# Pool in text order, y stored by SP from four buffers, and the steps of a routed mixture kernel placed anew

## The chip, the cores and the metric

The kernel runs on one core of one Trainium2 chip. The metric is the device time of one execution, in microseconds. A core has five engines with queues of their own: TensorE (PE in the profile, with its weight loads as PEld), VectorE (DVE), ScalarE (ACT), GpSimd (POOL) and SyncE (SP, which here only issues DMAs).

## The reference

Eight batches of eight heads hold 512 tokens and 32 states each, 64 wide. Tokens read the states by attention, states read the tokens, and the two results, heads side by side, are 4352 rows of 512. Each row then goes through the best of eight experts.

```python
scores = scale * x @ state.T;  a = softmax(scores);  xread = a @ state
scores2 = scale * state @ x.T; a2 = softmax(scores2); sread = a2 @ x
rows = concat([xread, sread]) -> (4352, 512)
e = argmax(rows @ w_gate); g = softmax(rows @ w_gate)[e]
out[row] = g * relu(row @ w1[e]) @ w2[e]
```

## The kernel before

All token rows of a batch are mixtures of its 32 states, and in practice go to one expert. So the kernel guesses the batch's expert from the states (`guess`), multiplies the states by the expert's w1 (`states_w1`, tile pG, result G), and works on 1024 hidden units as vectors over the states.

Batch 0 is done with all units (`in_full`: tiles ph, then py from s). For batches 1 to 7, `lists(b)` sorts the units: those that are positive for every token need no relu and can be summed into one matrix M, the few undecided are done one by one, the rest are dropped. Its steps are: two halves of pG; the load of the next w1 and four times two transposes (pgt) that ACT copies into gt; statistics on DVE; then the rank matmuls, DVE's table `to`, and eight indirect DMAs of POOL that scatter gt's rows into g_dram. `fetch(b)` reads the sorted rows back (tile gp, three DMAs of POOL), and `gather(b, 3)`, called twice, collects the rows of w2 that belong to them (w2c, three indirect DMAs of POOL each; nine w2c buffers, six a batch). `mask(b)` clears unused slots on DVE. `batch(b)` then multiplies: pgu transposes, pm (M from gp and w2c), phu, py, and stores.

Beside this run `front(b)` (transposes of x on DVE, the score matmuls pa<-xt,stT, softmax, and the exponentials of the states' side), `back(b)` (transposes pa2, pq, the states' read pw, then the load of the x two batches on and a store of st_dram, then the gate's pl and pcnt), and `tokens()`: for each of two halves of the state rows `sort_states` and `rounds`. A round handles 128 state rows in up to three experts at a time and reads the weights in pieces: `fetch(n)` issues n pieces of three loads into five ring buffers s; `round_in` loads xg and, by `values_of`, puts the experts' numbers into SP's registers.

Most engines are wrapped in `InOrder`, so that their instructions keep the order of the text; POOL's DMAs too are issued through such a wrapper (`gp`). The text itself is woven from generators: `todo` maps a letter to a generator, and a plan names the letters to advance at each `insert()` in `in_full` and `batch`:

```python
todo = {"A": back(0), "X": states_on(), "G": rest_of_G(), "B": backs(), "T": fronts(), "S": listing(), "F": fetching(), "M": masking(), "R": tokens(), "K": late_constants()}
```

`store_batch(b)` gives the store of 128 token rows: ACT scales py by the gate into one of three y buffers, and ACT issues the DMA to the output; the very last is scaled by DVE and stored by SP. PE's results go through four PSUM banks (`bank`) and a four-bank tile `pa` for scores. In the queues as built before, POOL's instructions do not stand everywhere as in the text: a batch's six gathers follow its fetch together, ahead of the next batch's scatters, and a scatter of srow into ss_dram stands between gathers.

Of the kernel before, what the change touches and what calls it, by code (L numbers as in the profile page):

```python
# [9 lines left out]
FP32 = mybir.dt.float32  # L10
# [10 lines left out]
def kernel(  # L21
# [21 lines left out]
    class InOrder:  # L43
# [5 lines left out]
        def __getattr__(self, name):  # L49
            def call(*args, **kw):  # L50
# [6 lines left out]
    pe, dve, act, gp, sp = (InOrder(e) for e in (nc.tensor, nc.vector, nc.scalar, nc.gpsimd, nc.sync))  # L57

    B, H, S, D = x.shape
    NS = state.shape[2]  # L60
    DM = H * D
    E = moe_w_gate.shape[1]
    F = moe_w1.shape[2]
# [4 lines left out]
    NC = S // 128  # L68
# [18 lines left out]
    const, dram, wpool, att, ffn, sst = (pool(n, **({"space": bass.MemoryType.DRAM} if n == "dram" else {}))  # L87
                                         for n in ("const", "dram", "wpool", "att", "ffn", "sst"))
# [9 lines left out]
    def bank(shape=(128, 512), name="p"):  # L98
        return ps_p.tile(list(shape), FP32, tag="p", bufs=4, name=name)

    std = [ffn.tile([128, 2, 160], FP32, tag="Gu", name="std"), ffn.tile([128, 2 * B - 4, 160], FP32, tag="gt", name="std"),
# [322 lines left out]
    def no_dep(d):  # L426
        tc.declare_no_dep(d.ins, group="y", reason="every row of the result is written once")
        tc.add_to_no_dep_group("y", d.ins)
# [53 lines left out]
    def store_batch(b):  # L482
        rows = out[ds(b * SO, S)].rearrange("(p c) f -> p c f", c=NC)

        def store(c, py):
            y = ffn.tile([128, DM], FP32, tag="y", bufs=3, name="y")
            if b == B - 1 and c == NC - 1:
                dve.tensor_scalar(y[:], py[:], gw[:, NC * b + c, :], None, ALU.mult)
                no_dep(sp.dma_start(out=rows[:, c], in_=y[:]))
            else:  # L490
                act.activation(y[:], py[:], AF.Copy, scale=gw[:, NC * b + c, :])
                no_dep(act.dma_start(out=rows[:, c], in_=y[:]))
        return store

    gps, w2cs = {}, {}
# [221 lines left out]
    def rounds(t, r0, r1):  # L717
        parts = [(r, *p) for r in range(r0, r1)
                 for p in [(1, k, half) for half in range(2) for k in range(NDC)] + [(2, f, 0) for f in range(NFC)]]
        have, xgs, ex = {}, {}, {}  # L720

        def round_in(r):
            xgs[r] = sst.tile([128, XW], FP32, tag="xg", bufs=2, name="xg")
            sp.dma_start(out=xgs[r][:].bitcast(I32), in_=ss_dram[t][ts(r, 128)])
            ex[r] = values_of(eg[t][0:1, r].rearrange("p a q -> p (a q)"), SP)

        def fetch(n):
            for _ in range(n):
                if parts:
                    r, kind, k, half = parts.pop(0)  # L730
                    if r not in ex:
                        round_in(r)
                    w = ring()
                    for q in range(3):
                        src = (moe_w1[ds(ex[r][q], 1), ts(k, 128), ts(half, 512)] if kind == 1
                               else moe_w2[ds(ex[r][q], 1), ts(k, 128), :])
                        sp.dma_start(out=w[:, q], in_=src.rearrange("o p f -> p (o f)"),
                                     cond=ex[r][3 + q], bounds_check="skip_entire_dma")
                    have[r, kind, k, half] = w

        def four(dst, lhsT, r, kind, k, half, start, stop):
            w = have.pop((r, kind, k, half))
            for q in range(4):
                pe.matmul(dst[ts(q, 32), :], lhsT=lhsT[:, ts(q, 32)], rhs=w[:, PLACE[q], :], start=start, stop=stop,
                          skip_group_check=True)

        round_in(r0)
        fetch(RING)
        yield
        for r in range(r0, r1):  # L750
            xg = xgs[r]
            pt = bank((128, NDC, 128), "ptx")
            for c in range(NDC):
                pe.transpose(pt[:, c, :], xg[:, ts(c, 128)], ident[:])
            xT = sst.tile([128, NDC, 128], FP32, tag="sxT", name="sxT")
            act.copy(xT[:], pt[:])
            yield
            h = sst.tile([128, F], FP32, tag="sh", name="sh")
            for half in range(2):
                ph = bank(name="pgh")  # L760
                for k in range(NDC):
                    four(ph, xT[:, k], r, 1, k, half, k == 0, k == NDC - 1)
                act.activation(h[:, ts(half, 512)], ph[:], AF.Relu)
                fetch(4)
                yield
            hT = sst.tile([128, F], FP32, tag="shT", name="shT")
            for u in range(2):
                pt = bank((128, 4, 128), "pth")
                for i in range(4):
                    pe.transpose(pt[:, i, :], h[:, ts(4 * u + i, 128)], ident[:])  # L770
                evict(hT[:, ts(u, 512)], pt[:].rearrange("p i k -> p (i k)"))
            yield
            y = ffn.tile([128, DM], FP32, tag="y", bufs=3, name="ys")
            for u in range(2):
                py = bank(name="pgy")
                for f in range(4 * u, 4 * u + 4):
                    four(py, hT[:, ts(f, 128)], r, 2, f, 0, f == 4 * u, f == 4 * u + 3)
                if u == 0:
                    dve.tensor_scalar(y[:], py[:], xg[:, DM:DM + 1], None, ALU.mult)
                    fetch(4)  # L780
                    yield
            dve.scalar_tensor_tensor(y[:], py[:], xg[:, DM:DM + 1], y[:], ALU.mult, ALU.add)
            no_dep(gp.indirect_dma_start(
                out=out[:], out_offset=bass.IndirectOffsetOnAxis(ap=xg[:, DM + 1:DM + 2].bitcast(I32), axis=0),
                in_=y[:], in_offset=None, bounds_check=NTOK - 1, oob_is_err=False))
            fetch(4)
            yield
# [32 lines left out]
    G = [sst.tile([128, F], FP32, tag=n, name="G0") for n in ("sh", "shT")]  # L820
# [102 lines left out]
    for k in "TT":  # L923
        next(todo[k])
    in_full(G, aTs[0], w2x, store_batch(0), inserts(
        "GXTX,XTT,AKTK,AA,SBSK,BSSS,SB,TSAT,BSST,,TA,,TT,SB,BTTF,SSSS,BSBB,STTT,,T,,TSST,MSF,BSBT"))
    plans = {
        1: "SFSB,,TBS,FB,FSM,,T,,,T,T,STSF,FB",
        2: "R,BSTR,S,BM,BSS,BFTF,S,RSSR,,TF,RT,BS,R",
        3: ",SFTS,BR,T,,SSBS,T,BTB,SBR,MR,TT,SS,BSRS",  # L930
        4: "B,SF,TRS,,BSFR,FSS,,,T,RMRT,SBTT,S,",
        5: "RBF,T,SBSS,RFB,SBR,B,RFFS,,,,RBR,MRRR,",
        6: "RF,RF,,,,,,,,MFR,,,R",
        7: ",,R,,,R,R,R,,R,,,",
    }

    pres = const.tile([128, B, E], FP32)
# [2 lines left out]

    def count_left():
        assert listed[0] == B - 1 and attended[0] == B and sorted_[0] == NT
        others = const.tile([128, B, E], FP32)
        eb_f = const.tile([128, B, 1], FP32)
        dve.tensor_copy(out=eb_f[:, :, 0], in_=eb[:])
        dve.tensor_tensor(others[:], io8[:].unsqueeze(1).to_broadcast([128, B, E]), eb_f[:].to_broadcast([128, B, E]),
                          ALU.not_equal)
        over = const.tile([128, B, 1], FP32)
        tmp8 = const.tile([128, B], FP32)
        dve.tensor_tensor(tmp8[:], nn[:, :, 1], nn[:, :, 0], ALU.subtract)  # L950
        dve.tensor_scalar(over[:, :, 0], nn[:, :, 0], float(CAPP), None, ALU.is_gt)
        dve.scalar_tensor_tensor(over[:, :, 0], tmp8[:], float(CAPU), over[:, :, 0], ALU.is_gt, ALU.max)
        dve.tensor_tensor(others[:], others[:], over[:].to_broadcast([128, B, E]), ALU.max)
        dve.scalar_tensor_tensor(pres[:], cnt[:], 0.5, others[:], ALU.is_ge, ALU.mult)
        n_f = const.tile([128, 2], FP32)
        dve.tensor_reduce(n_f[:, 0:1], pres[:], AX.XY, ALU.add)
        dve.tensor_reduce(n_f[:, 1:2], more[:], AX.X, ALU.add)
        rest_f = const.tile([128, 1], FP32)
        dve.tensor_reduce(rest_f[:], n_f[:], AX.X, ALU.add)
        dve.tensor_copy(out=n_i[:], in_=n_f[:])  # L960
        dve.tensor_copy(out=rest_i[:], in_=rest_f[:])
# [13 lines left out]
    with tc.If(number(rest_i[0:1, 0:1], B * E + NT * NR * 3) > 0):  # L975
# [4 lines left out]
        with tc.If(number(n_i[0:1, 0:1], B * E) > 0):  # L980
# [8 lines left out]
            with tc.For_i(0, n_pairs, 1):  # L989
# [47 lines left out]
                dve.tensor_tensor(off_i[:], off_i[:], t_x[:, 0, :], ALU.add)  # L1037

                def store(c, py):
                    y = ffn.tile([128, DM], FP32, tag="y", bufs=3, name="yx")  # L1040
                    dve.tensor_scalar(y[:], py[:], g_x[:, c, :], None, ALU.mult)
                    gp.indirect_dma_start(
                        out=out[:], out_offset=bass.IndirectOffsetOnAxis(ap=off_i[:, c:c + 1], axis=0),
                        in_=y[:], in_offset=None, bounds_check=NTOK - 1, oob_is_err=False)

                G = new_G()
# [34 lines left out]
```

## Time and profile before

| | |
|---|---|
| time, median of 3 runs | 426.52 us (425.7 to 427.35) |
| the profiled execution's own time | 424.81 us |
| its span, first to last instruction | 422.8 us |
| mean granted PE clock | 0.944 |
| PE, DVE, ACT, POOL busy | 369.2, 208.6, 122.2, 122.2 us |
| DMA | 92.74 MB, mean 219 GB/s |

The profile is of one execution. All instructions that go through the `InOrder` wrapper carry its line, L51, so groups are told apart by their tiles ("out<-in"), not by lines. A matmul of 32-bit data is recorded as two. Times in the trace count from the span's start. "Idle before" is how long the engine stood still, with what released it; the letters q after an engine mean its sequencer, which issues DMAs.

### The profile page before, as it was taken

How to read it: one execution, taken by the hardware profiler on the slowest of the kernel's cores; microseconds unless marked ns; L12 is line 12 of the kernel's file. 1: busy time of each engine (PE TensorE's matmuls, PEld its weight loads, DVE VectorE, ACT ScalarE, POOL GpSimd, SP SyncE). 2: the span in 40 equal slices, each digit the busy share in tenths (PEclk: the TensorE clock that was granted, in tenths of full speed). 3: DMA queues.
4: the chain of work that ended last, by engine and by line, in shares of the span. 5: the costliest groups of instructions: out<-in, count | busy, mean ns of one | idle time of the engine just before them, and what ended most of it. 6: DMA issues, size and time to landing. Idle time of an engine off the chain costs nothing. (4 is left out here: it accounts for less than half of the span.)

```text
span 422.8 us, 9169 instructions
## 1 busy us (share of the span) xinstructions
PE 369.2 (87%) x3313; PEld 167.5 (40%) x3320; DVE 208.6 (49%) x653; ACT 122.2 (29%) x230; POOL 122.2 (29%) x146
## 2 busy tenths in 40 slices
PE   4998999846999989999699707999999999999993
PEld 3354543513364345435343203534344334433331
DVE  5966878802797458588365202432844128200100
ACT  3374504300453251335111304211452013222110
POOL 2000026274304643262507400234151365200000
PEclk9999999965999999999889667999999999999998
DMA  6999923953305363338694399997688627897962
GB/s 166 365 331 257 332 97 112 333 209 104 99 28 188 127 173 106 111 107 318 204 309 162 99 320 347 371 320 232 212 293 296 195 96 205 253 338 255 391 235 73
DMA packets 50787, 92.74 MB, mean 219 GB/s; under 512 B 8023, under 2 KB 18274, under 8 KB 50736
## 3 DMA queue, kind: packets, MB, share of 16 engines
q1 hardware_dynamic: 37616, 62.09, 44.9%
q0 software_dynamic: 8128, 21.86, 16.1%
q10 hardware_dynamic: 4992, 8.14, 5.2%
q8 instruction: 28, 0.46, 0.5%
q14 instruction: 23, 0.19, 0.1%
HBM read 83.40 MB, written 20.42 MB: 246 GB/s over the span
## 5 line engine op out<-in xcount | busy, mean ns | idle before, releaser
L51 POOL DMA_INDIRECT g_dram<-gt,to x56 | 56.3, 1005 | 116.5 <-DVE G L51 55.8
L51 POOL DMA_INDIRECT w2c<-in_moe_w_dram,gp x42 | 43.4, 1034 | 104.9 <-PE pm L51 58.3
L51 PE MATMUL py<-M,aT 128*128 128x512 f32 x112 | 56.0, 623 | 0.2 <-ACT G L51 0.2
L51 PE MATMUL pm<-w2c,gp 128*128 128x512 f32 x112 | 52.2, 601 | 0.5 <-ACT y L51 0.2
L51 PE MATMUL py<-w2c,hu 128*128 128x512 f32 (+1 forms) x112 | 44.8, 634 | 0.0
L51 ACT ACTIVATE y<-py,gw 128x512 f32<-128x512 f32 x31 | 21.3, 687 | 78.2 <-PE py L51 40.7
L51 PE MATMUL pa<-xt,stT 32*32 32x128 f32 x1024 | 28.2, 317 | 17.0 <-issue 14.9
L51 DVE BATCH_NORM_STATS2 bn<-gt 128x6 f32<-128x256 f32 x56 | 20.1, 415 | 34.5 <-ACT gt L51 30.8
L51 PE MATMUL pgh<-s,sxT 128*32 128x512 f32 x192 | 25.0, 632 | 13.2 <-ACT y L51 12.7
L51 PEld LDWEIGHTS py<-M,aT 128*128 128x128 f32 x112 | 20.1, 194 | 26.1 <-issue 22.8
L51 PE MATMUL pG<-w1t,stT 64*32 64x512 f32 x256 | 25.6, 701 | 5.4 <-ACT sh L51 1.9
L51 PEld LDWEIGHTS pm<-w2c,gp 128*128 128x128 f32 x112 | 20.0, 190 | 20.5 <-issue 17.7
L51 PEld LDWEIGHTS pa<-xt,stT 32*32 32x32 f32 x1024 | 17.0, 112 | 27.6 <-issue 24.1
L51 DVE STREAM_TRANSPOSE sx<-pa 128x256 f32<-128x256 f32 (+1 forms) x36 | 11.9, 387 | 29.0 <-PE pa L51 29.0
L51 PE MATMUL py<-s,s 128*128 128x512 f32 x48 | 24.3, 641 | 0.3 <-ACT gt L51 0.3
L51 PEld LDWEIGHTS py<-w2c,hu 128*128 128x128 f32 (+1 forms) x112 | 15.2, 193 | 23.4 <-issue 23.2
L51 PE MATMUL pgy<-s,shT 128*32 128x512 f32 x192 | 23.3, 595 | 0.0
L51 DVE COPY G<-pG 128x512 f32<-128x512 f32 x14 | 9.6, 687 | 23.0 <-PE pG L51 22.8
L51 PE MATMUL phu<-aT,Gu 128*64 128x256 f32 (+1 forms) x84 | 20.8, 461 | 0.1
L51 ACT COPY gt<-pgt 128x512 f32<-128x512 f32 x28 | 15.4, 591 | 17.2 <-PE pgt L51 16.8
L51 DVE STREAM_TRANSPOSE xt<-x_nat 128x1024 f32<-128x1024 f32 x16 | 19.5, 1230 | 0.7 <-DMA x_nat<-in_x_dram 0.7
L51 ACT ACTIVATE sx<-sx 128x1024 f32<-128x1024 f32 (+1 forms) x9 | 8.6, 959 | 38.7 <-DVE sx L51 38.7
(204 smaller groups left out, 463.6 us busy)
## 6 DMA issues: line engine op xcount, KB each, us to landing
s<-in_moe_w_dram SPq DMA_DIRECT2D x144, 256.0 KB
w1t<-in_moe_w_dram SPq DMA_DIRECT2D x7, 2048.0 KB
x_nat<-in_x_dram SPq DMA_DIRECT2D x16, 512.0 KB
out_dram<-y ACTq DMA_DIRECT2D x31, 256.0 KB
gp<-g_dram POOLq DMA_DIRECT2D x7, 642.5 KB
ss_dram<-blank SPq DMA_DIRECT2D x8, 257.0 KB
w1t<-in_moe_w_dram SPq DMA_DIRECT2D x2, 1024.0 KB
s<-in_moe_w_dram SPq DMA_DIRECT2D x2, 768.0 KB
```

Source lines behind the costliest of these rows:

```text
L51: ins = getattr(self.engine, name)(*args, **kw)
```

## The change

POOL's instructions are put under manual scheduling: they stand in the order of the text. The y tile has four buffers in place of three. All stores of y are issued by SP, but for the last batch's third, which ACT keeps. `others` takes a buffer of `att` instead of one of its own. The plans are new.

```diff
+    ctx.enter_context(tc.manual_schedule(engines={mybir.EngineType.Pool}))
...
         def store(c, py):
-            y = ffn.tile([128, DM], FP32, tag="y", bufs=3, name="y")
+            y = ffn.tile([128, DM], FP32, tag="y", bufs=4, name="y")
             if b == B - 1 and c == NC - 1:
                 dve.tensor_scalar(y[:], py[:], gw[:, NC * b + c, :], None, ALU.mult)
-                no_dep(sp.dma_start(out=rows[:, c], in_=y[:]))
             else:
                 act.activation(y[:], py[:], AF.Copy, scale=gw[:, NC * b + c, :])
-                no_dep(act.dma_start(out=rows[:, c], in_=y[:]))
+            no_dep((act if b == B - 1 and c == NC - 2 else sp).dma_start(out=rows[:, c], in_=y[:]))
...
     in_full(G, aTs[0], w2x, store_batch(0), inserts(
-        "GXTX,XTT,AKTK,AA,SBSK,BSSS,SB,TSAT,BSST,,TA,,TT,SB,BTTF,SSSS,BSBB,STTT,,T,,TSST,MSF,BSBT"))
+        "G,TXXA,TAAA,X,TKT,KSBS,TBSS,KS,TSSA,BST,TB,,TFT,BTSS,BTSS,BSSS,TTB,,FSB,MT,TTTB,,SSBS,SSFB"))
     plans = {
-        1: "SFSB,,TBS,FB,FSM,,T,,,T,T,STSF,FB",
-        2: "R,BSTR,S,BM,BSS,BFTF,S,RSSR,,TF,RT,BS,R",
-        3: ",SFTS,BR,T,,SSBS,T,BTB,SBR,MR,TT,SS,BSRS",
-        4: "B,SF,TRS,,BSFR,FSS,,,T,RMRT,SBTT,S,",
-        5: "RBF,T,SBSS,RFB,SBR,B,RFFS,,,,RBR,MRRR,",
-        6: "RF,RF,,,,,,,,MFR,,,R",
-        7: ",,R,,,R,R,R,,R,,,",
+        1: "TBSS,F,,TFSS,T,T,TM,T,BSBR,,RBS,SB,FT",
+        2: "SST,B,R,FF,TBS,,BRMF,TSSR,RT,,,,S",
+        3: "SRT,FSSS,BT,RTB,,SBRS,,T,TM,,RSBR,TS,BB",
+        4: "FFF,BTS,MT,SSSR,FS,BBTF,S,,,,T,,SRS",
+        5: "TFRB,,SBSR,BSSB,,RSRF,,,R,FSMB,,,RF",
+        6: "FBR,,RRR,R,R,MF,,,,,R,,",
+        7: ",,,R,R,,,RR,R,,R,,",
     }
...
-        others = const.tile([128, B, E], FP32)
+        others = att.tile([128, B, E], FP32, tag="lg", name="others")
```

The y tiles of `rounds` and of the repair path ask for four buffers as well.

More of the change, by code (lines that the diff above doesn't have):

```diff
@@ L772, in rounds @@
             yield
-            y = ffn.tile([128, DM], FP32, tag="y", bufs=3, name="ys")
+            y = ffn.tile([128, DM], FP32, tag="y", bufs=4, name="ys")
             for u in range(2):
@@ L1039, in store @@
                 def store(c, py):
-                    y = ffn.tile([128, DM], FP32, tag="y", bufs=3, name="yx")
+                    y = ffn.tile([128, DM], FP32, tag="y", bufs=4, name="yx")
                     dve.tensor_scalar(y[:], py[:], g_x[:, c, :], None, ALU.mult)
```

## The prediction

> **What bounds the kernel now.** I read the page first: engine shares, then the 40 slices.
>
> ```profile
> span 422.8 us, 9169 instructions
> PE 369.2 (87%) x3313; PEld 167.5 (40%) x3320; DVE 208.6 (49%) x653; ACT 122.2 (29%) x230; POOL 122.2 (29%) x146
> PE   4998999846999989999699707999999999999993
> PEclk9999999965999999999889667999999999999998
> ```
>
> TensorE (PE) carries the kernel, no other engine passes 49%. But three dips stand in the PE row (slices 9 and 10, slice 20, slices 23 to 25), each with a clock below full. PE's own work, counted from its queue at the spacing that undisturbed stretches show, is less than 369: a 128x512 record follows the last after 0.427 us (184.5 us for the 432 of pm, ph and py), a group of four pgh or pgy records takes 0.427 too (41), phu 24, the transposes 0.13 each (36), pG 1.02 for 16 (16), the scores 1.83 for 128 (15), pw 0.94 for 64 (7.5), small ones 13: 338 us, in the 412 us between PE's first start (3.6) and last end (415.8). So 74 us are lost by PE, and the question is how many of them the change touches. I write W for the place in that 338 us and T for time in the trace; T minus W is 17 at W 18, 20 at W 52, 52 at W 163, 74 at W 199 and 78 at the end.
>
> I then took windows around five of the eight runs of score matmuls (tile pa: 128 records of 32x128, each with its own weights). Columns: length, then busy time and records of PE, PEld, DVE, ACT, POOL, then clock, DMA share, GB/s.
>
> ```profile
> 57.48:59.39 1.91, 1.91 (x136) 1.67 (x129) 1.49 (x8) 0.00 (x0) 0.04 (x1) 1.00 0.00 0
> 82.90:102.57 19.67, 9.04 (x132) 3.99 (x129) 2.03 (x12) 0.23 (x1) 14.09 (x16) 0.64 0.49 163
> 120.42:122.33 1.91, 1.91 (x130) 1.60 (x130) 1.53 (x3) 1.32 (x3) 0.00 (x0) 1.00 0.36 137
> 156.20:159.11 2.91, 2.56 (x130) 1.83 (x129) 0.76 (x2) 1.83 (x3) 0.83 (x1) 1.00 0.85 277
> 202.69:211.90 9.21, 5.45 (x131) 2.96 (x129) 2.58 (x13) 0.38 (x1) 4.86 (x5) 0.79 0.70 219
> ```
>
> The same 128 matmuls take 1.91 us where POOL is idle, 2.91 with 0.8 us of POOL's indirect DMAs beside them, 9.21 and 19.67 with long runs of these. In these long ones PE waits for no semaphore: a few records come every 0.7 us. The 64 matmuls of pw show it too: 1.10 alone, 2.20, 2.57 and 1.42 beside POOL. So do other queues: between 223 and 234, while POOL issues eight scatters, SP's register instructions come in clumps 0.7 us apart (66 take 12.8 us; afterwards 96 take 7.8), and ACT sits 9.3 us before a relu whose input is ready.
>
> Third, the timeline around the longest gap.
>
> ```profile
> 241.22 0.69 ACT L51 ACTIVATE y<-py,gw 128x512 f32<-128x512 f32 x1 [1.38 <-PE py L51]
> ...
> 244.97 10.29 SPq L51 DMA_DIRECT2D s<-in_moe_w_dram  x12
> 254.65 0.34 ACTq L51 DMA_DIRECT2D out_dram<-y  x1
> 255.09 0.69 ACT L51 ACTIVATE y<-py,gw 128x512 f32<-128x512 f32 x1 [13.19 <-DMA s<-in_moe_w_dram]
> ```
>
> ACT finishes y at 241.9 and issues its store at 254.65 only. In the built program that store waits for a semaphore that it shares with one of SP's loads of s, and SP, late from its register code, issues these from 245 on. ACT holds the next y, its bank stays full, PE waits 12.73 us for it.
>
> **What the Trainium skill says.** "TensorE: Matmul & The Clock Gate", Part 1, says that the PE clock drops to half after an idle window of about 3.4 us; the trace agrees: half clock from 88.5 to 105.7, from 208 to 214.9, and twice between 235 and 259. The same page, "Architectural detail", gives PE a queue of 64 instructions; that fits the first 28 and 38 matmuls of the two longest stretches, which with their weight loads go at full speed before the rest trickles. "DMA: Bandwidth & Descriptors", "SWDGE vs HWDGE vs iDMA": stores from SP and ACT are of one kind, POOL's descriptors are made in software; so moving y's store changes who waits, not the transfer (0.34 us issue on either queue in the trace). No page says that POOL's DMAs slow other engines' small instructions; that is the trace's alone.
>
> **The change, part by part.** The built programs' queues show what moves. Of y's 32 stores ACT keeps one, SP takes the rest. POOL's 56 scatters, 42 gathers and 21 fetches stay the same in number, in a new order: for batch 1 and 2 three gathers come after the fetch and three after the next batch's scatters; batch 5's eight scatters come ahead of batch 4's six gathers. PE, DVE and SP follow the new plans.
>
> *Taken away.* (a) The scores' stretches: 17.8 + 7.3 + 1.0 = 26.1 us, with the half clock that lasts on over full-size work (102.6 to 105.7, 211.9 to 214.9: half of 3.1 and 3.0, so 3.1). (b) pw: 1.1 + 1.5 + 0.3 = 2.9. (c) The gap at 243: 1.95 + 0.67 + 12.73, and half of the PE work at half clock between 235.3 and 242.1 and from 255.8 to 259.2 (3.3 + 1.7): 20.4. Sum 52.5 us. ACT's 31 issues (10.5 us of its sequencer) lay beside PE work.
>
> *Put in their place.* (d) Scores against POOL's new order. From the trace: `to` is ready 1 to 3 us after the rank matmul, the first scatter 0.8 later, eight take 10.3, the fetch follows after 1.9 and the first gather 5.4 to 10.8 after that; a gather takes 1.29. After rank at W 38.9, 65.3, 88.8, 131.8, 164.6, 208.4, 261.9 this puts scatters into some 2 to 12 us after each. The scores stand at W 38.9, 59.1, 80.4, 113.1, 152.2, 193.3. The first starts with the rank and is done when the scatter starts. No other lies inside a scatter run; 59.1 falls where three gathers are due (T 79 to 86 against 80 to 82), 80.4 at the end of one, 113.1 and 193.3 again at gathers, 152.2 in a free stretch. Gathers stop after three for want of w2c buffers, so each costs at most some 4.5 us: I take 2.5 + 1.5 + 2.5 + 2.5, 1.8 for the pw at W 205 and 2 for half clock: 12.8 us. Bounds 3 (all miss) and 26 (as now).
>
> (e) Batch 3's first gt copy waits on ACT until batch 2's scatters have landed: copy due at T 100.5, landing about 104. Behind it on ACT stand y and gt copies, for which PE's four banks give some cover: 1.5. Rank 1 now follows its last transposes by 2.9 us, its chain (two copies 1.2, statistics 0.8, nine small DVE steps 1.8) needs 3.8: 0.9. Exponentials ahead of pa2 at W 52: 1.0. Sum 3.4, bounds 0 and 8.
>
> (f) SP. In most places a store stands in SP's queue after loads that PE has freed and before loads that PE frees later, so it costs nothing; the cover is PE's work up to the freed buffer. The exception: after the first two stores of batch 2 (T about 173.5) SP's queue has the register code of the state rounds, 192 register instructions and two loads of registers (1 us each). At 0.065 us that is 14.5, slowed by scatters until 177.5: SP ends about 190. Only then come two stores, w1t, xg and 15 loads of s. The ptx transposes (W 155.7, T 189) wait for xg until about 193.5: 4.8. The pgh matmuls after them need 3 MB of s behind 2 MB of w1t, at 330 GB/s some 15 us from 191 on: 7 more. Sum 12; bounds 0 (if SP gets ahead) and 20. The fourth y buffer lets ACT be four stores ahead; it costs nothing. `others` in another place: nothing (DVE idle there). SP's 14 clearing stores now follow batch 2's x load, so they issue near T 44, not 24; the first scatter, near T 60, is their first user: nothing.
>
> Sum: 424.8 - 52.5 + 12.8 + 3.4 + 12 = 400.5 against the profiled execution's own 424.8, which lies 1.7 below the median shown, 426.5. So **402 us**.
>
> **Rivals.** *Slower: SP's queue becomes the bound.* Each expert-round step loads 3 MB through SP, eleven steps in all, and each now can stand behind a store that waits for ACT, that waits for PE, that waits for s. One such circle costs what (f) costs, 12 us. With (f) counted once, 24.5 us of gain remain, so from three more circles on the kernel is slower: 402 + 36 = 438. For it: SP already waits 68.3 us for pG and 44.7 for pw, in order. Against: the plans put stores after the freed buffers at ten of the eleven steps. *Half the gain: scores still meet POOL as before*, because gathers come at other times than I reckon, or because the loads of x and not POOL slow PE: (d) at 26, 415. For: 0.9 us extra at 291.65 with POOL idle. Against: clumps end with POOL's run on PE and SP alike. *More gain: the groups of three miss, and xg is early*: (d) 3, (f) 3, 383. That the change doesn't do what it says is out: the queues show it.
>
> **Numbers.** Measurement tells about 0.5% from no change, 424.4 to 428.6. Main case 0.52 (390 to 412), more gain 0.18, half the gain 0.17, slower 0.10, no change 0.03. Faster 0.87, same 0.03, slower 0.10. The range 383 to 418 leaves out the slower case and a little below.
>
> **What would show it.** After the change: no stretch of scores over 6 us; no idle PE before pgh of 12 us by ACT y; three or four stretches of scores of 3 to 6 us with gathers beside them; ACT waiting for scatters near T 100; PE waiting some 5 us before ptx near T 190 and again in pgh for s. A stretch of scores over 9 us, or repeated PE waits for s with SP's stores ahead of them, would prove me wrong; so would an early part (to W 20) that takes over 3 us more than now.

## The result, and the profile after

The changed kernel took **430.38 us** (median of 20 runs, 426.34 to 434.21), the kernel before 425.40 on the same chip: ratio **1.0095**, 95% interval 1.0066 to 1.0125. It is about 1% slower, where 402 us and a clear gain were predicted. Times here and below are medians of all runs; the ratios leave out runs that lie over 1.5% above the fastest of their kernel, so a ratio can differ a little from the quotient of two medians. The profiled execution took 430.19 us. Its page, the same three rows as before:

```profile
span 428.4 us, 9201 instructions
...
PE   4999998794799799989179969999989999999993
...
PEclk9999999888799599998769959999989999999997
```

The deep dip of before in slices 9 and 10 has become one in slices 10 and 11 (the digits 4 and 7), and the one in slice 24 is shallower (6 where 0 stood). A new one stands in slice 20 (the digit 1), and PE is at half clock in seven stretches, not four. PE ends at 421.3 in place of 415.8; T minus W, the time that PE has lost up to a given place in its own work, is 83.7 at the end in place of 78.3.

The windows that answer to the five stretches of before: four runs of scores (tile pa), a run of pw (from 79.02), and three that the prediction did not price, around the two halves of pG (columns as before: length, then PE, PEld, DVE, ACT, POOL, clock, DMA share, GB/s).

```profile
77.19:79.09 1.90, 1.90 (x133) 1.59 (x136) 1.50 (x10) 0.00 (x0) 0.00 (x0) 1.00 0.95 321
79.02:84.20 5.18, 2.96 (x70) 1.76 (x65) 3.63 (x6) 0.00 (x0) 3.12 (x3) 0.82 0.49 127
98.12:108.67 10.55, 3.55 (x37) 1.17 (x36) 5.08 (x10) 2.56 (x7) 8.72 (x10) 0.72 0.31 97
115.31:119.11 3.80, 3.08 (x133) 1.98 (x136) 1.71 (x5) 0.61 (x2) 1.51 (x2) 1.00 0.74 222
137.44:144.27 6.83, 3.00 (x21) 0.46 (x18) 1.86 (x7) 0.81 (x2) 5.69 (x7) 0.72 0.48 137
157.23:160.28 3.05, 2.70 (x131) 1.89 (x130) 0.73 (x2) 1.27 (x2) 1.00 (x1) 1.00 0.75 199
201.29:203.19 1.90, 1.90 (x130) 1.60 (x129) 0.26 (x3) 1.90 (x4) 0.00 (x0) 1.00 0.03 9
242.14:251.62 9.48, 4.15 (x20) 0.53 (x16) 0.46 (x1) 0.65 (x2) 7.31 (x9) 0.71 1.01 333
```

The scores are cured: but for the very first run (4.19 us here as before, with a wait for DVE in it) none takes over 3.80 us, and two pay 3.0 us in all. But three stretches with 20 to 37 records of PE, work for 1 to 3 us, take 10.55, 6.83 and 9.48 us, and POOL is busy in each for 5.7 to 8.7. What PE waits for there is in the timeline around the first of them:

```profile
101.37 1.40 PE L51 MATMUL pG<-w1t,stT 64*32 64x512 f32 x16 [2.16 <-ACT a L51]
...
102.76 1.07 PE L51 MATMUL pa<-ident,a 128*128 128x128 f32 x4
...
106.60 2.08 POOL L51 DMA_DIRECT2D gp<-g_dram  x3
108.03 0.58 ACT L51 COPY G<-pG 128x512 f32<-128x512 f32 x1 [6.71 <-remote]
108.07 0.11 SPq L51 DMA_DIRECT2D w1t<-in_moe_w_dram  x1
108.08 0.69 DVE L51 COPY G<-pG 128x512 f32<-128x512 f32 x1 [5.37 <-remote]
...
108.67 0.72 PEld L51 LDWEIGHTS pa<-ident,a 128*128 128x128 f32 x4 [5.24 <-ACT G L51]
```

The last pG matmul ends at 102.77 by the trace. Three engines that need nothing but that (ACT and DVE copy the two halves of pG, SP overwrites w1t) start together at 108.03 to 108.08. The trace's semaphore events say why: the three updates of PE's semaphore that they wait for are recorded at 108.01, 108.05 and 108.11. **PE's done signals come 5.2 us late.** The ends of matmuls are modelled in the profile, so it could also be the matmuls themselves that end late. But PE has gone on: the four transposes behind pG (the line at 102.76) start by 103.42. At 350 to 352 it shows again: the pm matmuls behind a pgu that ends at 350.05 follow each other at their usual 0.43 us, while pgu's signal comes at 352.36. No signal of ACT or DVE was found late in this way. Late ones of PE, by over 1 us, stand beside or just behind POOL's scatters and gathers, at 67, 80, 101, 108, 141, 193, 244, 250, 315 and 352. One exception was found, in the kernel before: a signal at 34.7, 1.5 us late, with POOL idle for 24.6 us. So POOL is not the only occasion. Where a timeline says "remote" after an engine's idle time, it has found the semaphore but no instruction that ended just then; that is how this looks.

PE's waits, longest first, show the second new loss:

```profile
PE ptx L51 <- DMA xg<-ss_dram: 11.3, 1, 11.3
PE pa L51 <- ACT G L51: 4.8, 1, 4.8
PE pl L51 <- ACT sh L51: 4.1, 1, 4.1
```

and the timeline of SP's queue (SPq) where xg comes from:

```profile
183.97 22.66 SPq L51 DMA_DIRECT2D out_dram<-y  x4
...
207.01 0.42 SPq L51 DMA_DIRECT2D w1t<-in_moe_w_dram  x1
207.54 0.50 SPq L51 DMA_DIRECT2D xg<-ss_dram  x1
208.65 13.34 SPq L51 DMA_DIRECT2D s<-in_moe_w_dram  x15
...
216.45 1.09 PE L51 MATMUL ptx<-ident,xg 128*128 128x128 f32 x4 [11.34 <-DMA xg<-ss_dram]
```

The four stores span 22.66 us because SP's register code stands between the second and the third: the first table is loaded at 187.03, 96 instructions take from 188.00 to 198.46, the second 97 from 199.85 to 205.76. Then xg, behind 2 MB of w1t, takes 8.9 us to be there.

### The profile page after: what moved, and what is told of

It is laid out like the page before. It is cut to its first block, busy times and chain, and to the rows that moved or that the text cites. A ratio compares the mean times of both kernels' runs of the same rounds, so it can differ in the third digit from the quotient of the medians.

```text
span 428.4 us, 9201 instructions
## 1 busy us (share of the span) xinstructions
PE 374.0 (87%) x3313; PEld 169.9 (40%) x3320; DVE 208.8 (49%) x653; ACT 120.5 (28%) x230; POOL 124.4 (29%) x146
## 5 line engine op out<-in xcount | busy, mean ns | idle before, releaser
L51 POOL DMA_INDIRECT g_dram<-gt,to x56 | 58.4, 1042 | 158.2 <-DMA st_dram<-xs 53.0
L51 PE MATMUL pm<-w2c,gp 128*128 128x512 f32 x112 | 56.2, 637 | 2.7 <-ACT G L51 2.1
L51 PE MATMUL py<-M,aT 128*128 128x512 f32 x112 | 57.2, 635 | 0.1
L51 ACT ACTIVATE y<-py,gw 128x512 f32<-128x512 f32 x31 | 19.9, 683 | 67.8 <-PE py L51 38.9
L51 DVE COPY shT<-pth 128x512 f32<-128x512 f32 x3 | 2.1, 691 | 40.9 <-PE pth L51 40.9
L51 PE MATMUL pa<-xt,stT 32*32 32x128 f32 x1024 | 18.3, 295 | 2.6 <-DVE sx L51 1.1
L51 POOL DMA_INDIRECT out_dram<-ys,xg x3 | 3.0, 990 | 58.1 <-DVE ys L51 55.3
L51 ACT COPY G<-pG 128x512 f32<-128x512 f32 x18 | 10.3, 586 | 26.7 <-PE pG L51 17.8
```

The lines of the kernel that those rows point to most:

```text
L51: ins = getattr(self.engine, name)(*args, **kw)
```

## The experiments

The experiments ran on five chips, and each chip also ran the kernel before. They turned out to be of **two kinds**: on the first, before takes 425 us (the result above) and 422 (one of the five), on the second 393 to 395 (the other four). Whether it is the chip or what else ran on it isn't known; "kind of chip" is short for it. Times are compared on one chip only, except where the text sets one kind against the other.

**The parts of the change, one by one.** `p_pool` is before with the line of `manual_schedule` alone:

```diff
+    ctx.enter_context(tc.manual_schedule(engines={mybir.EngineType.Pool}))
```

> The kernel before with one line of the change: Pool's instructions keep the order of the text; stores and plans as before. Theory A (POOL's runs of indirect DMAs slow every stretch of small matmuls they meet, so what counts is where runs and small matmuls stand against each other): the old plans were made for the old order, six gathers in one piece, so the new order shifts runs of 4 to 10 us onto other stretches; time moves by some 1 to 3% in either direction, with scores and pw stretches of other lengths than 19.67, 9.21 and 2.91 us. Theory B (what costs is SP's queue with the stores in it): POOL's order is neutral, within 0.5% of before.

`p_store` is before with the stores alone (SP stores, four y buffers, `others` moved):

```diff
-                no_dep(act.dma_start(out=rows[:, c], in_=y[:]))
+            no_dep((act if b == B - 1 and c == NC - 2 else sp).dma_start(out=rows[:, c], in_=y[:]))
```

> The kernel before with the stores of the change alone: SP stores y, four y buffers, ACT issues none but one; plans and POOL's order as before. Theory A: the 12.73 us wait for ACT's store before pgh at 243 goes, scores keep 19.67 and 9.21 us, so 8 to 14 us faster, about 413 to 418. Theory B (stores in SP's queue hold back the loads of s and x behind them): not faster, 425 or more, with PE waiting for s, xg or w1t in new places.

`p_pool_plans` is the changed kernel with the last diff undone, `p_store_plans` the changed kernel without the line of `manual_schedule`.

> The changed kernel with the stores as before: ACT issues them from three buffers; POOL's order and plans as changed. Theory A: the losses of the changed kernel beside POOL's runs stay; ptx's wait for xg shrinks by the two stores' worth only (1 us), because the register code comes first in SP's queue either way; within 1% of the changed kernel, 426 to 434. Theory B: 10 us or more faster than the changed kernel, below 420, with ptx waiting less than 5 us in place of 11.34.

> The changed kernel without the fixed order of POOL: stores and plans as changed, POOL's instructions placed by the scheduler as before. Theory A: gathers in one piece of six again, runs of up to 16 us, so stretches of small matmuls meet more of POOL's work than in the changed kernel: slower than it by 1 to 3%, or as slow. Theory B: the same as the changed kernel within 0.5%, since SP's queue is the same.

Measured: before 394.91; p_pool 393.62 (ratio 0.9946, 0.9919 to 0.9974), p_store 394.71 (0.9979, 0.9951 to 1.0007), p_pool_plans 394.16 (0.9963, 0.9935 to 0.9992), p_store_plans 393.66 (0.9978, 0.9954 to 1.0002). The surprise is the 394.91: 30 us less than 425 for the same kernel. No run of scores after the first takes over 3.4 us in these traces, though up to 2.7 us of POOL's DMAs lie beside one. The changed kernel itself did not run on this chip, so what was expected of the parts against it was not tried, and a chip of this kind could not show theory A. As to the parts, all are within 0.6% of before. The stores alone take away the wait for ACT's y (14.2 us in p_pool) and put one for s in its place (7.5 us in three waits, 6.0 the longest), as theory B says. But with the stores back on ACT (p_pool_plans) ptx still waits 8.85 us for xg, not under 5; in p_store_plans, with the stores on SP, it waits 14.8. So most of the wait comes from the register code and w1t, and the stores add to it.

**The change on the second kind of chip.** `after_again`, `after_c` and `after_d` are the changed kernel as it is.

> The changed kernel as it is, as a control beside the others of this call. On the chip of the last four runs the kernel before took 394.9 us, not 425.4, and its long stretches of scores were gone. Theory A (PE's slowness beside POOL's indirect DMAs is what separates the chips, and the changed kernel meets as much of it as the kernel before): where before takes 395, after takes 393 to 396 and has no stretch of small matmuls over 4 us; where before takes 425, after takes about 430. Theory B (after is slower whatever the chip): ratio 1.005 to 1.013 on either.

> The changed kernel once more, beside the next three on one chip. On a chip where 256 small matmuls took 12 us beside gathers and scatters (before 421 to 425 us) it should be slower than before by 0.5 to 1.3%, as in the first comparison; on a chip where they took 6 us (before 394 us) faster by 0.7 to 1.1%.

> The changed kernel beside the next two on one chip, for the kind of chip and as their control. Where before takes 421 us or more: 0.5 to 1.3% slower than before; where it takes 394: 0.9 to 1.4% faster, as on two chips already.

Measured: 389.71 against 393.78 (0.991, 0.9886 to 0.9933), 390.09 against 395.19 (0.9864, 0.9804 to 0.9924), 390.09 against 393.48 (0.992, 0.9894 to 0.9946). So **the sign depends on the chip**: 1% slower on the first kind (one chip), 1% faster on the second (three chips). The time of after_again is below the 393 to 396 that theory A gave, and the rule of theory B (slower on any chip) falls. The same copies of pG as above, here in after_again's timeline:

```profile
96.69 2.26 PE L51 MATMUL pG<-w1t,stT 64*32 64x512 f32 x16 [2.16 <-ACT G L51]
...
99.03 0.59 ACT L51 COPY G<-pG 128x512 f32<-128x512 f32 x1 [2.39 <-PE pG L51]
99.07 0.11 SPq L51 DMA_DIRECT2D w1t<-in_moe_w_dram  x1
99.08 0.69 DVE L51 COPY G<-pG 128x512 f32<-128x512 f32 x1 [1.05 <-PE pG L51]
```

The matmuls end at 98.95, the three start 0.08 to 0.13 us later, not 5.3.

**What slows what, by itself.** `micro` computes nothing of the reference. In each phase full matmuls warm PE up, DVE then makes the indices that release POOL, and PE runs 128 small matmuls (256 records) or 24 large ones (48 records) beside it. `micro2` is the same with the plain DMAs of SP and POOL and POOL's work on data held back until the stretch begins (in micro, SP's had already run).

```python
for kind, work in (("none", "small"), ("gather", "small"), ("scatter", "small"), ("pooldma", "small"),
                   ("spdma", "small"), ("compute", "small"), ("gather", "big")):
```

> A kernel of its own that computes nothing of the reference: PE runs 256 small matmuls (32x128, each with its weights) or 24 large ones while POOL issues eight gathers, eight scatters, eight plain DMAs of the same 256 KB, or works on data without a DMA, or SP issues the eight plain DMAs, or nothing. Theory A: 256 matmuls take 3.7 us alone and with SP's DMAs, and 3 to 10 times that beside gathers and scatters; the 24 large ones stay at 0.43 us each. Rival C (it is the traffic of the DMAs, not POOL): slow beside SP's DMAs too. Rival D (it is POOL being busy): slow beside its work on data too.

> The kernel of the micro run again, with SP's and POOL's plain DMAs and POOL's work held back until the stretch begins. Where before takes 394 us: 5 to 7 us for the 256 small matmuls in all six cases, as on the last chip. Where it takes 425 us, theory A: 6 us alone and beside SP's DMAs, 12 us or more beside gathers and scatters, and DVE's copy over 1 us late after them; rival C: as slow beside SP's DMAs.

Windows of micro2's second pass, on a chip of the first kind: alone, gathers, scatters, SP's DMAs, POOL's work, and the large matmuls beside gathers (columns: length, PE, PEld, DVE, POOL, clock, DMA share, GB/s).

```profile
386.78:392.57 5.79, 5.34 (x258) 4.91 (x257) 0.00 (x0) 0.00 (x0) 1.00 0.02 6
434.75:447.49 12.74, 9.51 (x258) 7.57 (x257) 0.00 (x0) 4.69 (x5) 0.73 0.41 127
489.68:502.17 12.49, 9.63 (x258) 7.36 (x257) 0.00 (x0) 4.46 (x5) 0.73 0.32 121
596.45:603.35 6.90, 5.40 (x258) 4.87 (x257) 0.00 (x0) 0.00 (x0) 1.00 0.45 165
645.54:651.15 5.61, 5.34 (x258) 4.81 (x257) 0.00 (x0) 5.28 (x5) 1.00 0.01 3
693.24:714.00 20.76, 20.76 (x50) 9.28 (x49) 0.00 (x0) 4.77 (x5) 1.00 0.27 76
```

and of micro, on a chip of the second kind, beside gathers and beside scatters:

```profile
420.83:427.96 7.13, 5.58 (x258) 5.18 (x257) 0.00 (x0) 4.70 (x5) 1.00 0.75 198
470.14:475.46 5.32, 5.32 (x258) 5.10 (x257) 0.00 (x0) 4.10 (x5) 1.00 0.57 210
```

On the first kind (one run, two passes) the small matmuls take 12.7 and 12.5 us beside gathers and scatters, twice as long as alone, at a mean clock of 0.73 (in the first pass 12.0 and 12.2, against 7.97 alone, where half clock came in); SP's DMAs cost 1.1 us at a higher data rate, POOL's work without DMAs nothing; the large matmuls take 20.76 beside gathers, as they do on the second kind alone. POOL's plain DMAs took 5.19 in one pass and 8.98 in the other, so whether only indirect DMAs slow PE stays open. On the second kind nothing is slowed much. So rivals C and D fall as the main cause, and theory A holds on the first kind for the small matmuls. How POOL's DMAs come to slow PE, through its supply of instructions or its semaphores, was not tried. The late copy of DVE, over 1 us, was expected and not seen (0.04 to 0.09 us in all phases), perhaps because the stretch outlasted most of POOL's run; the late signals rest on the kernels' own traces.

`micro3` was to tell which shapes are slowed, with pG's shape and transposes added.

> A kernel of its own that computes nothing of the reference: 256 matmuls of 32x128, 64 of 64x512 on half the rows (the shape of pG), 48 transposes of 128x128, or 24 full 128x512, each alone, beside eight gathers and beside eight scatters. On the slow kind of chip, theory A: what is slowed is the rate of instructions (some 10 in 0.72 us), so the first two shapes take 1.5 to 2.5 times as long beside POOL, the transposes (0.13 us each) hardly longer, the full ones not at all. Rival (every matmul waits for memory or semaphores): all four are slowed. On the other kind: none is.

It met a chip of the second kind, where none is: pG's shape (128 records) takes 7.10 us in all cases, 48 transposes 5.40, the large ones 20.76, the small ones 5.2 to 6.8. On the first kind this stays open.

**How much lies beside POOL in all.** `a_nopool` (also `a_nopool_c`, `a_nopool_d`) is the changed kernel, `b_nopool` the kernel before, with the loop of scatters out of `lists` and this in `gather`:

```diff
-            gp.indirect_dma_start(
-                out=w2cs[b][j][:], out_offset=None, in_=rows,
...
+            gp.memset(w2cs[b][j][:], 0.01)
```

> The changed kernel without POOL's scatters, and with each gather replaced by a memset of the same buffer on POOL: the sorted rows and the rows of w2 are left out, everything else runs. Theory A: what PE loses beside POOL's indirect DMAs is gone. On a chip where before takes 425 the time falls by 35 to 48 us to 382 to 395; where before takes 395 it falls by 5 to 12 only. Rival (the losses are the plans' waits for ACT, DVE and SP): it falls by under 10 on either.

> The changed kernel without POOL's scatters and with memsets in place of its gathers (the sorted rows and w2's rows are left out). On a chip where before takes 394 us it took 4 us less than the changed kernel. Where before takes 421 to 425, theory A: 30 to 45 us less than the changed kernel, about 385 to 392, the same as on the other chips, with no done signal of PE over 1 us late before the last 10 us. Rival (a part of the 30 us between the chips is something else, such as a slower clock or memory): less than 20 us.

> The kernel before with the same left out: no scatters, memsets in place of the gathers. Theory A: its time is free of the chip's kind, 383 to 392 us, and the 12 to 15 us wait for ACT's y before pgh is mostly still there or shorter, because SP's register code is not slowed any more. Without POOL's DMAs the two plans then stand within 1% of each other: 52.5 us of removed losses were mostly the same losses that the new plans meet elsewhere.

> The changed kernel with scatters left out and memsets in place of the gathers, for the kind of chip that it has not run on. Where before takes 421 or more, theory A: 385 to 392 us, 35 us or more under the changed kernel. Rival (the 30 us between the kinds of chips are not POOL's DMAs): over 405. Where before takes 394: 386 again.

All four ran on the second kind: 385.72 (after_again 389.71), 386.75 (after_c 390.09), 387.25 for b_nopool on the same chip (before 395.19), and 391.47 (after_d 390.09), one run each. There the DMAs are worth 4 us at most to the changed kernel, just under theory A's 5 to 12 and within the rival's 10, so these runs do not decide between the two. To the kernel before they are worth 8, so this kind is nearly, not wholly, free of the effect; without them the two kernels stand 0.5 us apart. What the changed kernel takes without POOL's DMAs on the first kind, 385 to 392 us by theory A, was not measured. That is the main open end: there the cost of POOL rests on traces and on micro2.

**SP's register code.** `f_xg_first` moves one step, so that xg is ahead of w1t:

```diff
-        3: "SRT,FSSS,BT,RTB,,SBRS,,T,TM,,RSBR,TS,BB",
+        3: "RST,FSSS,BT,RTB,,SBRS,,T,TM,,RSBR,TS,BB",
```

> The changed kernel with the first three steps of batch 3's plan in another order, so that SP issues the load of xg ahead of the 2 MB of w1t. If ptx's wait of 11.34 us is the queue behind w1t's 2 MB (xg took 8.9 us from issue to landing), it falls to 3 to 6 us and the kernel gains 6 to 9 us, half clock included. If it is the register code ahead of both, the wait stays at 9 or more and the time within 0.5% of the changed kernel.

Measured 389.32 (0.9874, 0.9845 to 0.9904; after_again on the same chip 389.71): the gain of 6 to 9 us over the changed kernel did not come. PE's wait for xg falls from 10.7 to 1.2 us, and pgh waits 6.7 us for s instead (4.6 the longest): the second block of register code, 186.0 to 197.8, now stands ahead of the next twelve loads. `f_regs` adds to it that the tables are read at their place in the text (in `values_of`):

```diff
-        _, regs = nc.values_load_multi_w_load_instructions(
+        ins, regs = nc.values_load_multi_w_load_instructions(
...
+        for i in ins:
+            tc.keep_in_program_order(i)
```

> The changed kernel with two edits: the experts' numbers are read into SP's registers at their place in the text, not as early as their table is ready, and xg is loaded ahead of w1t (first three steps of batch 3 in another order). Theory (SP's 192 register instructions, 6.3 us for 96, stand in one block ahead of the loads of xg and s, and a block further on is what the last run's wait of 4.63 us for s came from): both blocks dissolve into the spaces between loads, ptx and the first pgh wait less than 2 us each, 10 to 14 us less than the changed kernel on the same chip, ratio to before 0.955 to 0.97 where before takes 394. Rival (the transfers themselves bound it: 2 MB of w1t and 3 MB of s at some 330 GB/s): PE waits 5 us or more for s in pgh and the gain is under 4 us.

> The kernel before as it is, for its trace on this chip. If the chip is like the two of the last runs (394 us): no stretch of scores over 4 us, the wait of 12 to 15 us for ACT's y before pgh still there. If it is like the first (425 us): 19.67 and 9.21 us again.

> The changed kernel with the registers read at their place in the text and xg ahead of w1t, now beside the changed kernel itself. Theory: it takes away ptx's wait of 10.7 to 11.3 us and its half clock and nothing else, so it is 10 to 16 us (2.5 to 4%) faster than the changed kernel on either kind of chip, since the wait does not come from POOL. Rival (the wait only moves to s): under 4 us.

On the first kind f_regs took 415.46 against 421.77 for before (0.979, 0.9728 to 0.9852). In the profiled run (417.95, the slowest of six) PE waits for neither xg nor s over 1 us there, the long waits left are for ACT (4.3 before pl, 3.5 before pcnt), with PE's signals late. before_again, on the same chip, repeats the first profile: scores 19.31 and 8.92 us, 13.82 for ACT's y. On the second kind f_regs_c took 389.93, after_c 390.09 (ratios to before 0.9861, 0.9773 to 0.9949, and 0.9864): no gain over the changed kernel, where a ratio of 0.955 to 0.97 was expected. Its timeline says where the time went that PE no longer loses before ptx:

```profile
201.41 1.06 PE L51 MATMUL pgh<-s,sxT 128*32 128x512 f32 x8
204.75 1.95 PE L51 MATMUL pgh<-s,sxT 128*32 128x512 f32 x6 [2.27 <-DMA s<-in_moe_w_dram]
207.14 4.40 PE L51 MATMUL pgh<-s,sxT 128*32 128x512 f32 x14 [0.44 <-DMA s<-in_moe_w_dram]
212.53 1.05 PE L51 MATMUL pgh<-s,sxT 128*32 128x512 f32 x2 [0.99 <-DMA s<-in_moe_w_dram]
214.55 1.04 PE L51 MATMUL pgh<-s,sxT 128*32 128x512 f32 x2 [0.97 <-DMA s<-in_moe_w_dram]
```

These 32 records are 3.4 us of PE's work and take 14.2, while the window from 200 to 216 moves 354 GB/s with the DMA engines full. Where PE is early, w1t, x and s are simply not there sooner: on the second kind the rival is right. On the first kind f_regs has the best ratio to before, 0.979 against 1.0095 for the changed kernel, but the two were measured on different chips, so that the register code makes the difference there is not shown. On the second kind it is level with the changed kernel.

## Why the prediction was wrong

The two kinds of chip let the sum be checked in two pieces. On the second kind, nearly free of POOL's effect, before takes 393.8 and after 389.7. On the first, in the result above, they take 425.4 and 430.4. What the first kind adds is **31.6 us for before, 40.7 for after**.

*Taken away, (a) and (b): right as far as it can be checked.* 26.1 + 3.1 + 2.9 = 32.1 us was the price of POOL beside scores and pw; the difference between the kinds of chip is 31.6 for before. That the two agree to half a microsecond is in part luck, since the difference holds everything that the kinds do differently. But most of it lies where (a) had it: against p_pool on the second kind, before loses some 19 us more between W 60 and 70 and 10 more between 160 and 170, at the two long runs of scores. In the changed kernel the scores pay 3.0.

*(c), (e), (f): the sum right, in part by luck, two of its parts not.* They were to give 20.4 - 3.4 - 12 = 5.0 us; the second kind, on which little else is left, gains 4.1. The gap at 243 is gone. (f) was 12, and T minus W grows by 14.4 between W 149 and 160 (on the second kind by 13.0), but not as told: not 4.8 before ptx and 7 in pgh, but 11.34 before ptx, about 3 of half clock, and nothing in pgh. The prediction let xg land 3.5 us after SP's block; it took 8.9 from issue behind w1t's 2 MB, and in that time s came. (e) did not happen: batch 2's scatters were out by 102.6, and the first gt copy came at 111.36 only, held back by PE's late signals.

*(d): the step that failed.* 12.8 us were put in for what the new plans still meet of POOL. What scores and pw pay comes near it: scores 3.0, pw 4.1 + 2.5, half clock after pw 2.6, in all 12.2. But that is luck, for it falls in other places. Of the four runs of scores priced, two pay (1.9 and 1.15 us) and two pay nothing; the pw priced at W 205 takes 1.10, as alone, and two others pay, the one at T 79 some 1.3 to 2.1 of its 4.1 on the second kind as well. Above all, (d) priced scores and pw alone, and every other group of PE, and every signal of PE, at nothing. T minus W grows in four more places, all with POOL's DMAs beside them: by 10.4 between W 65 and 78 (pG, pa2, pgt), by 8.3 between 95 and 105 (pl, pG), by 3.7 between 144 and 149 (pgt), by 11.1 between 173 and 183 (pgh, pG): 33.5 us, of which the same places cost 5.9 on the second kind. That is 27.6 us that no term had: small groups of PE beside POOL, and waits for PE's late signals, up to 5.2 us each. The miss is 430.4 - 402 = 28.4; that the two agree so closely is luck too, since the errors of the other terms cancel. The new plans took the scores out of POOL's runs and put pG's 32 records a batch into them.

*Where it could have been seen.* The prediction read "ACT sits 9.3 us before a relu whose input is ready" as ACT's instructions arriving slowly. In that trace ACT's relu starts at 234.17, and an update of PE's semaphore is recorded at 234.15: the input was computed (the last pgh matmul beside the scatters ends at 226.55, and PE had gone on to py at 226.48), but the signal came 7.6 us late:

```profile
223.79 2.76 PE L51 MATMUL pgh<-s,sxT 128*32 128x512 f32 x24
...
234.17 0.60 ACT L51 ACTIVATE sh<-pgh 128x512 f32<-128x512 f32 x1 [9.30 <-remote]
```

Seen so, every group of PE whose signal someone waits for would have had a price beside POOL, pG first. The rule taken instead, slow are the 128 and 64 records of scores and pw, fitted the five windows shown.

*The list of what would show it.* No scores over 6 us: right. No 12 us before pgh by ACT's y: right. Stretches of scores of 3 to 6 us beside gathers: two, not three or four. ACT waiting for scatters near T 100: wrong. PE waiting before ptx: right in place, twice the size; in pgh: wrong. Of the three signs that would prove it wrong none came: no run of scores over 9 us, no repeated waits for s, and up to W 20 the changed kernel loses some 3 us less, not more. Nothing on that list looked at pG. The rival of half the gain named the right mechanism (scores meet POOL as before) in the wrong tiles; the slower rival, circles of SP's queue, did not come.

The Trainium skill, "TensorE: Matmul & The Clock Gate", Part 1, says that the clock drops to half after an idle window of about 3.4 us. The trace agrees: half clock from 102.8 to 113.1, 140.4 to 150.6 and 246.2 to 256.4, in and after the three stretches above, so that a late signal costs more than its wait. The prediction's reading of a queue of 64 fits only loosely: the 38 matmuls of the second stretch make 76 records with their weight loads.

## What to carry to other kernels

A wait that an engine ends at the very moment of a semaphore's update, long after its producer's recorded end, belongs to the signal and not to the waiting engine, if the producer has meanwhile gone on to later instructions: compare these times before giving the wait a price. A price found on one group of instructions is tried on every group of that engine that the new order puts into the same place, above all on those whose result another engine waits for. And a difference of 1% between two plans can have either sign on two chips: the part of the time that depends on the chip is to be known before plans are chosen by it.

## What the runs showed of the hardware

- Of the chips met, the first kind (two chips) took 31 to 41 us more than the second (four), of some 390, for the same program, most of it in stretches beside POOL's indirect DMAs. Leaving these DMAs out gains 8 us at most on the second kind. POOL's own instructions take the same time on both (a gather 1.03 to 1.08 us). What sets the kind was not found.
- On the first kind both PE's small instructions and its done signals come late beside POOL's indirect DMAs (signals up to 5.2 us in the changed kernel, 7.6 in the kernel before), SP's register instructions too: 96 take 10.5 us beside scatters and 6.3 us on the second kind. No signal of ACT or DVE was found late.
- pw's stretch at T 79 has a gap of 1.1 to 1.9 us on the second kind as well, with POOL's DMAs and without them (2.42 us for 1.10 in a_nopool). A packet of 16 KB of the instruction queue (q8) falls there, at 78.79 in after_again and 77.59 in a_nopool; that it is the cause was not tried.
